# Biased scores in SBUF with one minimum per half tile, weights in three DVE passes with their low halves by the tensor engine, feed-forward six half tiles behind

## The chip, the core and the metric

The kernel runs on one core of a Trainium2 chip. A core has a tensor engine (TensorE, in the profile PE, its weight loads PEld), a vector engine (VectorE, DVE), a scalar engine (ScalarE, ACT), GpSimd (POOL) and SyncE (SP), whose queue issues all DMAs here. The metric is the device time of one execution in microseconds; each kernel is timed in several runs, and one more execution is profiled.

## What is computed

The inputs q, k and v have 8 batches, 8 heads, 576 positions and 64 values per head, in fp32. The feed-forward weights arrive as 64-bit floats.

```python
scores = scale * q @ k^T                        # scale = 1/8
scores = where(0 <= row - col < 128, scores - slope_h * |row - col|, -1e9)
attn = exp(scores - max(scores)); attn = attn / (sum(attn) + 1e-9)
x = (attn @ v), heads side by side              # 8 x 576 x 512
h = relu(x @ w_in)                              # 512 -> 1024
gate = sigmoid(3-tap convolution of h along the sequence, per channel)
out = (h * gate) @ w_out                        # 1024 -> 512
```

## The kernel before

All 8 x 576 positions lie in one row of 4608 and are cut into 36 tiles of 128. Two tiles make a chunk of 256 columns for the feed-forward, so there are 18 chunks. Heads come in two units u of four; "half tile" stands for one unit of a tile in the attention, and for one of the two slots of an iteration in the feed-forward.

Attention, per tile t and unit u. `qkT` transposes q and k on TensorE (`pt`) and copies them out (L219). `scores` multiplies them in plain fp32 into two PSUM banks `sc`, against the tile itself and the tile before. DVE folds the two together by mask copies (L246; in tiles that contain a batch boundary two more of them per bank), and then, head by head, one fused instruction (L261) scales by -1/8, adds the bias in place in PSUM and leaves the row minimum in `st`. ScalarE reads the bank, takes the exponential into `e` and leaves its sum (L271). DVE adds 1e-9, inverts (L279, L280) and scales `e` (L281). `attnT` transposes `e` on TensorE (`pa`), ScalarE copies it out (L291), GpSimd cuts it into the parts for this tile and the one before (L294, L297). `av` of tile t - 1 runs one iteration later; its result is split into a rounded high half `x[:,0]` (L323, ScalarE) and a low half `x[:,1]` (L324, DVE). `xfin` then copies one column between neighbouring chunks, since the convolution reaches one position to each side: for an even tile the first column of the new chunk into the last column of the chunk before (L338), for an odd tile the other way (L340).

Feed-forward, per chunk and pair of 128-channel blocks (four such items per chunk, 72 in all). `up` multiplies x by w_in in three products of halves into banks `p`, 24 matmuls; ScalarE and DVE make relu, convolution and gate (`hh`, `z`, L365 to L380), then `gh` (L385) and `gl` (L386, GpSimd) are the halves of the result. `down` multiplies them by w_out into `o`, 12 matmuls. The banks `sc`, `pt`, `pa`, `av`, `p` share six PSUM buffers in rotation.

Weights. Each of 16 blocks of 128 x 512 (and the small convolution block) is fetched as pairs of 32-bit words into `wst` (three buffers), turned into fp32 in `wg` by `to_f32`, and split into a rounded high half (`wi[0]`, `wo[0]`, L177) and a low half (`wi[1]`, `wo[1]`, L178).

The order. TensorE's order is the order of the code (a manual schedule). The other engines' orders are made by a scheduler from priorities, and each engine then works strictly in its order. Iteration t issues: scores of tile t, `av` of tile t - 1 with `xfin`, loads, some weight blocks by the table WEIGHTS, the up of slot 2t, a down, `qkT` of tile t + 1, `pa` of unit 0, more weight blocks, the up of slot 2t + 1, `pa` of unit 1, a down. The item of slot s is number s - LAG. With LAG = 7 the first up of a chunk falls on the second slot of an odd iteration; the last column that it reads comes from the tile whose `av` stands at the head of the same iteration.

Of the kernel before, what the change touches and what calls it, by code (L numbers as in the profile page):

```python
# [8 lines left out]
F32 = mybir.dt.float32  # L9
F32R = mybir.dt.float32r  # L10
# [3 lines left out]
AF = mybir.ActivationFunctionType  # L14
ALU = mybir.AluOpType

P = 128
# [4 lines left out]
def tile_alibi_window_attention_conv_glu(  # L22
# [10 lines left out]
    nc = tc.nc  # L33
# [4 lines left out]
    HU = 4  # L38
# [8 lines left out]
    cpool = ctx.enter_context(tc.tile_pool(name="cpool", bufs=1))  # L47
# [3 lines left out]
    pst = ctx.enter_context(tc.tile_pool(name="pst", bufs=6, space=bass.MemoryType.PSUM))  # L51
    pso = ctx.enter_context(tc.tile_pool(name="pso", bufs=2, space=bass.MemoryType.PSUM))

    def as32(ap):
        return ap.bitcast(F32)


    ident_f = apool.tile([P, P], F32, name="ident_f", tag="e", bufs=2)
    make_identity(nc, ident_f)
    ident_r = cpool.tile([P, P], F32R, name="ident_r")  # L60
    nc.vector.tensor_copy(out=ident_r, in_=ident_f)
    ident = as32(ident_r)

    ones = apool.tile([P, P], F32, name="ones", tag="e", bufs=2)
    nc.vector.memset(ones, 1.0)
# [3 lines left out]
    def mask_from(name, conds):  # L69
# [19 lines left out]
        out=mh, in_=mh, pattern=[[0, P]], compare_op=ALU.is_ge, fill=0.0, base=-(P // 2), channel_multiplier=1  # L89
# [10 lines left out]
    dist = apool.tile([P, P], F32, name="dist", tag="qk", bufs=2)  # L100
    nc.gpsimd.iota(dist, pattern=[[-1, P]], base=0, channel_multiplier=1, allow_small_or_imprecise_dtypes=True)
    nc.vector.scalar_tensor_tensor(
        out=dist, in0=m_prev_f, scalar=float(P), in1=dist, op0=ALU.mult, op1=ALU.add
    )
    bias = cpool.tile([P, H, P], F32, name="bias")
    for h in range(H):
        slope = 2.0 ** (-8.0 * (h + 1) / H)
        nc.vector.tensor_scalar(
            out=bias[:, h, :], in0=dist, scalar1=-8.0 * slope, scalar2=None, op0=ALU.mult
        )  # L110


# [7 lines left out]
    WB = 512  # L120

    def to_f32(st, g):

        lo, hi = st[..., 0], st[..., 1]
        gf = g.bitcast(F32)
        nc.scalar.activation(out=g, in_=hi.bitcast(F32), func=AF.Tanh, scale=16513.0)
        nc.vector.tensor_scalar(
            out=lo, in0=lo, scalar1=29, scalar2=0x40000000, op0=ALU.logical_shift_right, op1=ALU.bitwise_or  # L130
        )
        nc.vector.tensor_scalar(
            out=hi, in0=hi, scalar1=4, scalar2=1, op0=ALU.logical_shift_left, op1=ALU.logical_shift_right
        )
        nc.vector.tensor_tensor(out=hi, in0=hi, in1=lo, op=ALU.bitwise_xor)  # L135
        nc.vector.scalar_tensor_tensor(
            out=gf, in0=hi.bitcast(F32), scalar=3.0e38, in1=g, op0=ALU.min, op1=ALU.mult
        )
        return gf
# [25 lines left out]
    def convert_weight():  # L165
        block, st = fetched.pop(0)
        g = wpool.tile([P, WB], I32, name="wg", tag="wg")
        if block is None:
            n = 3 * NFC
            f = to_f32(st, g[:n, :P])  # L170
            ps = pst.tile([P, n], F32, name="pcw", tag="tr")
            nc.tensor.transpose(ps, f, ident[:n, :n])
            nc.vector.tensor_copy(out=cw.rearrange("p k f -> p (k f)"), in_=ps)
            return
        f = to_f32(st, g)
        hi, lo = block[1]
        nc.scalar.copy(out=hi, in_=f)  # L177
        nc.gpsimd.tensor_tensor(out=lo, in0=f, in1=as32(hi), op=ALU.subtract)  # L178

# [2 lines left out]
    NG = HU // 2  # L184
# [36 lines left out]
    def scores(t, u):  # L221
        first = (t * P) % S
        slot = t % SLOTS
        if slot:
            win, prev, cur = slice(slot - 1, slot + 1), 0, 1
        else:
            win, prev, cur = slice(0, SLOTS, SLOTS - 1), 1, 0
        e = apool.tile([P, HU, P], F32, name=f"e{t}_{u}", tag="e", bufs=2)
        st = apool.tile([P, 3, HU], F32, name=f"st{t}_{u}", tag="st", bufs=3)

        pss = [pst.tile([P, NG, 2, P], F32, name=f"sc{t}_{u}_{a}", tag="tr") for a in range(2)]
        for g in range(NG):
            for a in range(2):
                rows = slice(a * D, (a + 1) * D)
                qt = qkT_all[rows, slot, u, 0, g, :]
                if first == 0:
                    nc.tensor.matmul(pss[a][:, g, cur], qt, qkT_all[rows, slot, u, 1, g, :], start=True, stop=True)
                else:
                    nc.tensor.matmul(pss[a][:, g], qt, qkT_all[rows, win, u, 1, g, :], start=True, stop=True)  # L239
        for a in range(2):  # L240
            ps = pss[a]
            s_cur, s_prev = ps[:, :, cur, :], ps[:, :, prev, :]
            shp = [P, 2, P]

            def put(mask, data):
                nc.vector.copy_predicated(  # L246
                    out=s_cur, mask=mask.unsqueeze(1).to_broadcast(shp), data=data
                )

            negb = neg.unsqueeze(2).to_broadcast(shp)  # L250
            if first == 0:
                put(m_prev, negb)
            else:
                put(m_prev, s_prev)
                if first + P > S:
                    put(m_half, negb)
                elif first < P:
                    put(m_after, negb)
            for g in range(NG):
                j = 2 * g + a  # L260
                nc.vector.tensor_tensor_reduce(  # L261
                    out=ps[:, g, cur, :],
                    in0=ps[:, g, cur, :],
                    in1=bias[:, u * HU + j, :],
                    scale=-0.125,
                    scalar=3.0e38,
                    op0=ALU.add,
                    op1=ALU.min,
                    accum_out=st[:, 0, j : j + 1],
                )  # L270
                nc.scalar.activation(  # L271
                    out=e[:, j, :],
                    in_=ps[:, g, cur, :],
                    func=AF.Exp,
                    bias=st[:, 0, j : j + 1],
                    scale=-1.0,
                    accum_out=st[:, 1, j : j + 1],
                )
        nc.vector.tensor_scalar(out=st[:, 2, :], in0=st[:, 1, :], scalar1=1e-9, scalar2=None, op0=ALU.add)  # L279
        nc.vector.reciprocal(out=st[:, 2, :], in_=st[:, 2, :])  # L280
        nc.vector.tensor_tensor(out=e, in0=e, in1=st[:, 2, :].unsqueeze(2).to_broadcast([P, HU, P]), op=ALU.mult)  # L281
        es[t, u] = e
# [133 lines left out]


    NFP = NFC // 2
    LAG = 7
    todo = [(c, i) for c in range(NCH) for i in range(NFP)]  # L420
    fns, downs = {}, []
    pos = 0
# [1 line left out]
    wpool = ctx.enter_context(tc.tile_pool(name="wpool", bufs=3))  # L424
    blocks = list(weight_blocks())

    WEIGHTS = [(0, 2), (1, 1), (1, 1), (1, 1), (2, 2), (2, 2), (2, 0)]

    def weight(n):
        for _ in range(n):  # L430
            if fetched:
                with tc.high_priority(WPRI):
                    convert_weight()
            if blocks:
                fetch_weight(blocks.pop(0))
# [3 lines left out]
    def up(slot):  # L439
        nonlocal pos  # L440
        if pos < len(todo) and pos + LAG <= slot:
            c, i = todo[pos]
            pos += 1
            if c not in fns:
                fns[c] = ffn_items(c)
            with tc.high_priority(-15):
                fns[c][0](i)
            downs.append((c, i))

    def down(keep=2):  # L450
        if len(downs) > keep:
            c, i = downs.pop(0)
            fns[c][1](i)
# [11 lines left out]
    with tc.manual_schedule(engines={mybir.EngineType.PE}):  # L465
        loads(0)
        for _ in range(3):
            fetch_weight(blocks.pop(0))
        loads(1)
        loadvs(0)  # L470
        for u in range(2):
            qkT(0, u)
        for t in range(NT + 2):
            if t < NT:
                with tc.high_priority(60):
                    for u in range(2):
                        scores(t, u)
            if 0 < t <= NT:
                av(t - 1)
                xfin(t - 1)  # L480
            loads(t + 2)
            loadvs(t + 1)
            wa, wb = WEIGHTS[t] if t < len(WEIGHTS) else (0, 0)
            weight(wa)
            up(2 * t)
            down()
            if t + 1 < NT:
                for u in range(2):
                    qkT(t + 1, u)
            if t < NT:  # L490
                with tc.high_priority(100):
                    attnT(t, 0)
            weight(wb)
            up(2 * t + 1)
            if t < NT:
                with tc.high_priority(100):
                    attnT(t, 1)
            down()
        while pos < len(todo):
            up(len(todo) + LAG)  # L500
            down()
        while downs:
            down(0)
# [28 lines left out]
```

## Time and profile before

| | |
|---|---|
| median of 3 runs | 690.79 us (689.79 to 690.88) |
| the profiled execution | 690.37 us |
| its span, first to last instruction | 688.6 us |
| mean granted TensorE clock | 0.960 |
| busy: PE, PEld | 630.3, 549.3 us |
| busy: DVE, ACT, POOL | 504.9, 444.8, 210.2 us |

Reading help. In the page's part 2 each digit is the busy share of a fortieth of the span, in tenths. A row of windows gives, for a stretch in us from the start, its length, each engine's busy time with the number of instructions, the granted clock (PEclk), the DMA share and the rate. A row of waits names the engine, tile and line that waited, what ended the wait, the total, the number of times and the longest. A timeline row gives start, duration, engine, line, operation, tiles, shapes and, in brackets, the idle time before it. Matmul rows run into each other, so the time from one start to the next is the time that counts. A plain fp32 matmul is recorded as two instructions.

### The profile page before, as it was taken

The page shows a single profiled execution, that of the slowest core. Times are in us where ns is not written, and L with a number is a line of the kernel's source. Part 1 is how long each engine was busy: PE and PEld are TensorE (multiplying, and loading weights), DVE is VectorE, ACT ScalarE, POOL GpSimd, SP SyncE. Part 2 cuts the span into 40 slices and gives each one's busy share as a digit, 9 for nine tenths or more (in the row PEclk, how much of TensorE's full clock was granted, in tenths as well). Part 3 has the DMA queues.
Part 4 walks back from the last instruction along what each step waited for, and adds up shares of the span by engine and source line. Part 5 has one row for each costly group of instructions (what it writes and reads, how often), then busy time and mean ns, then how long its engine had stood idle before and what let it go on. Part 6 is the DMA issues. An engine that isn't in the chain of part 4 may idle for free.

```text
span 688.6 us, 13622 instructions
## 1 busy us (share of the span) xinstructions
PE 630.3 (92%) x4833; PEld 549.3 (80%) x4833; DVE 504.9 (73%) x1584; ACT 444.8 (65%) x1258; POOL 210.2 (31%) x233
## 2 busy tenths in 40 slices
PE   3544499999999999999999999999999999999997
PEld 3333388888888888888888888888888888888996
DVE  6999887777777777777777677777777777777542
ACT  5554576766676667676667666767676667675563
POOL 1355433333232232322233333333232222323221
PEclk9566599999999999999999999999999999999999
DMA  9555322223222323222313222323222322000000
GB/s 228 140 187 164 78 47 47 79 47 78 62 62 47 79 46 79 47 77 47 93 31 78 47 77 48 78 47 78 62 62 47 79 47 77 17 31 1 31 32 30
DMA packets 120103, 47.03 MB, mean 68 GB/s; under 512 B 113356, under 2 KB 113380, under 8 KB 120036
## 3 DMA queue, kind: packets, MB, share of 16 engines
q1 hardware_dynamic: 120036, 46.17, 26.5%
q8 instruction: 38, 0.62, 0.4%
q14 instruction: 29, 0.24, 0.1%
HBM read 36.72 MB, written 9.44 MB: 67 GB/s over the span
## 4 chain that ended last, share of the span: by engine, by line
DVE 45%; PE 29%; ACT 20%; issue 3%; DMA 1%; POOL 1%; ACTq 0%; SPq 0%; DVEq 0%; POOLq 0%
DVE z L373 18%; PE p L360 11%; PE o L401 11%; DVE sc L246 7%; DVE sc L261 5%; ACT e L271 4%; ACT qkT_all L219 3%; DVE e L281 3%; ACT z L379 3%; DVE z L380 2%; PE sc L239 2%; PE av L315 2%; DVE x L324 2%; DVE wst L135 2%; ACT z L366 2%
## 5 line engine op out<-in xcount | busy, mean ns | idle before, releaser
L373 DVE SCALAR_TENSOR_TENSOR z<-hh,cw,z 128x256 f32<-128x256 f32 (+7 forms) x384 | 182.7, 518 | 96.8 <-ACT z L366 93.3
L360 PE MATMUL p<-x,wi 128*128 128x258 f32 x1728 | 230.9, 289 | 9.6 <-ACT e L271 7.6
L360 PEld LDWEIGHTS p<-x,wi 128*128 128x128 f32 x1728 | 215.5, 191 | 18.3 <-ACT e L271 11.0
L386 POOL TENSOR_TENSOR gl<-z,gh 128x512 fp32r<-128x512 f32 x72 | 92.6, 1286 | 382.7 <-ACT gh L385 339.4
L401 PE MATMUL o<-wo,gh 128*128 128x512 f32 x576 | 183.5, 400 | 0.0
L271 ACT ACTIVATE e<-sc,st 128x128 f32<-128x128 f32 x288 | 104.9, 368 | 44.6 <-DVE st L261 35.7
L379 ACT ACTIVATE z<-z 128x512 f32<-128x512 f32 x72 | 45.4, 631 | 117.4 <-DVE z L373 117.2
L401 PEld LDWEIGHTS o<-wo,gh 128*128 128x128 f32 x576 | 103.2, 188 | 19.5
L401 PE MATMUL o<-wo,gl 128*128 128x512 f32 x288 | 113.8, 395 | 0.0
L261 DVE CUSTOM_DVE_ANT_0 sc<-sc,bias 128x128 f32<-128x128 f32 x288 | 80.7, 302 | 12.2 <-ACT e L271 9.3
L380 DVE SCALAR_TENSOR_TENSOR z<-z,hh 128x512 f32<-128x512 f32 x72 | 50.1, 696 | 50.3 <-ACT z L379 50.3
L366 ACT ACTIVATE z<-hh,cw 128x256 f32<-128x256 f32 x144 | 73.8, 513 | 7.7
L288 PE MATMUL pa<-ident_r,e 128*128 128x128 f32 x288 | 46.2, 286 | 32.9 <-DVE e L281 26.0
L315 PEld LDWEIGHTS av<-rl,rv 128*64 128x64 f32 x1088 | 59.3, 138 | 13.3 <-issue 10.6
L315 PE MATMUL av<-rl,rv 128*64 128x128 f32 x1088 | 68.5, 278 | 0.9 <-POOL rl L297 0.8
L239 PE MATMUL sc<-qkT_all 64*128 64x256 f32 x512 | 68.8, 411 | 0.0
L401 PEld LDWEIGHTS o<-wo,gl 128*128 128x128 f32 x288 | 54.1, 188 | 13.0
L385 ACT CAST gh<-z 128x512 fp32r<-128x512 f32 x72 | 45.1, 627 | 29.0 <-DVE z L380 29.0
L239 PEld LDWEIGHTS sc<-qkT_all 64*128 64x128 f32 x512 | 49.9, 199 | 16.9 <-issue 10.8
L288 PEld LDWEIGHTS pa<-ident_r,e 128*128 128x128 f32 x288 | 35.0, 147 | 35.4 <-issue 7.7
L297 POOL TENSOR_SCALAR_AFFINE_SELECT rl<-rl 128x512 f32<-128x512 f32 x72 | 52.1, 724 | 35.5 <-ACT rl L291 31.3
L365 ACT ACTIVATE hh<-p 128x258 f32<-128x258 f32 x144 | 55.5, 385 | 9.0 <-PE p L360 8.5
(57 smaller groups left out, 632.1 us busy)
## 6 DMA issues: line engine op xcount, KB each, us to landing
out_dram<-ob SPq DMA_DIRECT2D x36, 256.0 KB, 2.1
rqk<-in_q_dram SPq DMA_DIRECT2D x32, 256.0 KB, 3.4
rqk<-in_k_dram SPq DMA_DIRECT2D x32, 256.0 KB, 3.8
rv<-in_v_dram SPq DMA_DIRECT2D x32, 256.0 KB, 3.0
wst<-in_moe_w_in_dram SPq DMA_DIRECT2D x8, 512.0 KB, 5.3
wst<-in_moe_w_out_dram SPq DMA_DIRECT2D x8, 512.0 KB, 3.5
rqk<-in_q_dram SPq DMA_DIRECT2D x8, 128.0 KB, 2.9
rqk<-in_k_dram SPq DMA_DIRECT2D x8, 128.0 KB, 3.2
```

Of the source, the lines that this page charges most:

```text
L239: nc.tensor.matmul(pss[a][:, g], qt, qkT_all[rows, win, u, 1, g, :], start=True, stop=True)
L261: nc.vector.tensor_tensor_reduce(out=ps[:, g, cur, :], in0=ps[:, g, cur, :], in1=bias[:, u * HU + j, :], scale=-0.125, scalar=3.0e38, op0= ...
L271: nc.scalar.activation(out=e[:, j, :], in_=ps[:, g, cur, :], func=AF.Exp, bias=st[:, 0, j : j + 1], scale=-1.0, accum_out=st[:, 1, j : j + 1],
L288: nc.tensor.transpose(ps[:, j, :], e[:, j, :], ident)
L315: nc.tensor.matmul(ps[a * D : (a + 1) * D, u * NG + g], vraw[tt][:, u * HU + j], rl[:, side, j], start=n == 0, stop=n == len(sides) - 1,)
L360: nc.tensor.matmul(ps[:, :XW], a[:, cc, f * P : (f + 1) * P], x[:, cc, :], start=n == 0, stop=n == last)
L366: nc.scalar.activation(out=z[:, ff, :], in_=hh[:, ff, 1 : 1 + CW], func=AF.Copy, scale=cw[:, 1, f : f + 1])
L373: nc.vector.scalar_tensor_tensor(out=z[:, ff, a:cut], in0=hh[:, ff, a + kk : cut + kk], scalar=cw[:, kk, f : f + 1], in1=z[:, ff, a:cut], ...
L379: nc.scalar.activation(out=z, in_=z, func=AF.Tanh)
L380: nc.vector.scalar_tensor_tensor(out=z, in0=z, scalar=1.0, in1=hh[:, :, 1 : 1 + CW], op0=ALU.add, op1=ALU.mult)
L386: nc.gpsimd.tensor_tensor(out=gl, in0=z, in1=as32(gh), op=ALU.subtract)
L401: nc.tensor.matmul(oo[m], g[:, ff, ms], w[:, f, :], start=f == 0 and n == 0, stop=f == NFC - 1 and n == 2)
```

## The change

Scores. The bias table now holds slope x distance instead of -8 times it. One scalar_tensor_tensor per bank (two heads) computes -1/8 x score + bias from PSUM into `e` in SBUF; one tensor_reduce per half tile takes the four minima; the exponentials then work in place in `e`.

Weights. `to_f32` gets a scaled copy on ScalarE (L131 of the new kernel) and has three DVE passes instead of four. The low half is no longer a subtraction on GpSimd: TensorE adds f (by the identity, in fp32) and -hi (by a negative identity, in fp32r) in a bank `pw`, and ScalarE copies it out.

Order. LAG is 6, the table WEIGHTS spreads the blocks otherwise, and the first down of an iteration stands ahead of its up.

```diff
+    nident = cpool.tile([P, P], F32R, name="nident")
+    nc.vector.tensor_scalar(out=nident, in0=ident_f, scalar1=-1.0, scalar2=None, op0=ALU.mult)
...
-        nc.scalar.activation(out=g, in_=hi.bitcast(F32), func=AF.Tanh, scale=16513.0)
-        nc.vector.tensor_scalar(
-            out=lo, in0=lo, scalar1=29, scalar2=0x40000000, op0=ALU.logical_shift_right, op1=ALU.bitwise_or
+        nc.scalar.activation(out=g, in_=hi.bitcast(F32), func=AF.Tanh, scale=1.0e9)
+        nc.scalar.activation(out=hi.bitcast(F32), in_=hi.bitcast(F32), func=AF.Copy, scale=2.0**-112)
+        nc.vector.tensor_scalar(out=lo, in0=lo, scalar1=29, scalar2=None, op0=ALU.logical_shift_right)
+        nc.vector.scalar_tensor_tensor(
+            out=hi, in0=hi, scalar=3, in1=lo, op0=ALU.logical_shift_left, op1=ALU.bitwise_or
         )
-        nc.vector.tensor_scalar(
-            out=hi, in0=hi, scalar1=4, scalar2=1, op0=ALU.logical_shift_left, op1=ALU.logical_shift_right
-        )
-        nc.vector.tensor_tensor(out=hi, in0=hi, in1=lo, op=ALU.bitwise_xor)
...
         nc.scalar.copy(out=hi, in_=f)
-        nc.gpsimd.tensor_tensor(out=lo, in0=f, in1=as32(hi), op=ALU.subtract)
+        ps = pst.tile([P, WB], F32, name="pw", tag="tr")
+        nc.tensor.matmul(ps, ident, f, start=True, stop=False)
+        nc.tensor.matmul(ps, nident, hi, start=False, stop=True)
+        nc.scalar.copy(out=lo, in_=ps)
...
-            for g in range(NG):
-                j = 2 * g + a
-                nc.vector.tensor_tensor_reduce(
-                    out=ps[:, g, cur, :],
-                    in0=ps[:, g, cur, :],
-                    in1=bias[:, u * HU + j, :],
-                    scale=-0.125,
...
-                    accum_out=st[:, 0, j : j + 1],
-                )
-                nc.scalar.activation(
-                    out=e[:, j, :],
-                    in_=ps[:, g, cur, :],
...
+            heads = e.rearrange("p (g a) k -> p a g k", a=2)[:, a]
+            b = bias[:, u * HU : (u + 1) * HU].rearrange("p (g a) k -> p a g k", a=2)[:, a]
+            nc.vector.scalar_tensor_tensor(out=heads, in0=s_cur, scalar=-0.125, in1=b, op0=ALU.mult, op1=ALU.add)
+        nc.vector.tensor_reduce(out=st[:, 0, :], in_=e, axis=mybir.AxisListType.X, op=ALU.min)
+        for j in range(HU):
+            nc.scalar.activation(
+                out=e[:, j, :],
+                in_=e[:, j, :],
...
-    LAG = 7
+    LAG = 6
...
-    WEIGHTS = [(0, 2), (1, 1), (1, 1), (1, 1), (2, 2), (2, 2), (2, 0)]
+    WEIGHTS = [(0, 2), (1, 1), (1, 0), (0, 3), (3, 2), (2, 2)]
...
             weight(wa)
+            down(1)
             up(2 * t)
-            down()
```

What moves on the engines, at the places that the prediction speaks of. First TensorE in iteration 7, where chunk 2 begins (its x is `x_699` before and `x_754` after; the numbers behind the names only count allocations). Before, behind the first slot's down:

```order
L401 MATMUL o_1_1328<-wo_113,gh_1_1233 128x512
L401 MATMUL o_1_1328<-wo_114,gh_1_1233 128x512
L401 MATMUL o_1_1328<-wo_113,gl_1_1234 128x512
L218 MATMUL pt_0_1462<-ident_r,rqk_1182 128x128 x4
L218 MATMUL pt_1_1468<-ident_r,rqk_1182 128x128 x4
L288 MATMUL pa_0_1474<-ident_r,e_0_1341 128x128 x4
L360 MATMUL p_0_1485<-x_699,wi_111 128x258 x2
```

After, the last rows of `av` of tile 6 and of the down that follows it, with the engines that a row waits for:

```order
L397 MATMUL o_0_1291<-wo_115,gh_2_1343 128x512
L397 MATMUL o_0_1291<-wo_116,gh_2_1343 128x512
L397 MATMUL o_0_1291<-wo_115,gl_2_1344 128x512
L397 MATMUL o_1_1292<-wo_115,gh_2_1343 128x512
L397 MATMUL o_1_1292<-wo_116,gh_2_1343 128x512
L397 MATMUL o_1_1292<-wo_115,gl_2_1344 128x512
L356 MATMUL p_0_1510<-x_754,wi_113 128x258 [waits DVE_49,Activation_49]
```

The first up of the chunk, p_0, moved from behind the transposes and pa of its iteration to right behind the first down.

Second, DVE in the same iteration, up to the copy of the column that this up reads. Before:

```order
L261 ISA sc_1_0_1364,st_1_1363<-sc_1_0_1364,bias 128x128
L261 ISA st_1_1363 128x1
L281 TENSOR_TENSOR e_0_1341<-e_0_1341,st_0_1342 128x512
L261 ISA sc_1_1_1365,st_1_1363<-sc_1_1_1365,bias 128x128
L261 ISA st_1_1363 128x1
L324 TENSOR_TENSOR x_1180<-av_1383,x_1180 128x4x128
L279 TENSOR_SCALAR st_1_1363<-st_1_1363 128x4
L338 CAST x_699<-x_1180 128x8
```

After:

```order
L265 TENSOR_REDUCE st_0_1432<-e_0_1431 128x4
L249 COPY_PREDICATED sc_1_0_1453<-m_prev,sc_1_0_1453 128x2x128
L249 COPY_PREDICATED sc_1_1_1454<-m_prev,sc_1_1_1454 128x2x128
L264 SCALAR_TENSOR_TENSOR e_1_1451<-sc_1_0_1453,bias 128x2x128
L264 SCALAR_TENSOR_TENSOR e_1_1451<-sc_1_1_1454,bias 128x2x128
L265 TENSOR_REDUCE st_1_1452<-e_1_1451 128x4
L275 TENSOR_SCALAR st_0_1432<-st_0_1432 128x4
L276 RECIPROCAL st_0_1432<-st_0_1432 128x4
L277 TENSOR_TENSOR e_0_1431<-e_0_1431,st_0_1432 128x512
L320 TENSOR_TENSOR x_1284<-av_1471,x_1284 128x4x128
L334 CAST x_754<-x_1284 128x8
```

The copy (L338, now L334) stays behind the scores of both units and the scaling of the first.

Third, TensorE at the end of iteration 0. Before:

```order
L218 MATMUL pt1_0_195<-ident_r_78,rqk1_131 128x128 x4
L218 MATMUL pt1_1_201<-ident_r_78,rqk1_131 128x128 x4
L288 MATMUL pa0_0_207<-ident_r_78,e0_0_148 128x128 x4
L288 MATMUL pa0_1_235<-ident_r_78,e0_1_169 128x128 x4
L239 MATMUL sc1_0_0_245<-qkT_all_116 128x256
```

After:

```order
L284 MATMUL pa0_0_207<-ident_r_78,e0_0_150 128x128 x4
L179 MATMUL pw_222<-wg_215,ident_r_78 128x512
L180 MATMUL pw_222<-wi0_113,nident_80 128x512
L179 MATMUL pw_235<-wg_228,ident_r_78 128x512
L180 MATMUL pw_235<-wi0_113,nident_80 128x512
L284 MATMUL pa0_1_241<-ident_r_78,e0_1_170 128x128 x4
L242 MATMUL sc1_0_0_251<-qkT_all_118 128x256
```

The products of the first two weight blocks stand between the two units' transposes. The other fourteen stand in iterations 1 (two), 3 (three), 4 (five) and 5 (four); the first up stands in iteration 3, behind `av` of tile 2.

More of the change, by code (lines that the diff above doesn't have):

```diff
@@ L108, in tile_alibi_window_attention_conv_glu @@
         nc.vector.tensor_scalar(
-            out=bias[:, h, :], in0=dist, scalar1=-8.0 * slope, scalar2=None, op0=ALU.mult
+            out=bias[:, h, :], in0=dist, scalar1=slope, scalar2=None, op0=ALU.mult
         )
@@ L258, in scores @@
                     put(m_after, negb)
-            for g in range(NG):
-                j = 2 * g + a
-                nc.vector.tensor_tensor_reduce(
-                    out=ps[:, g, cur, :],
-                    in0=ps[:, g, cur, :],
-                    in1=bias[:, u * HU + j, :],
-                    scale=-0.125,
-                    scalar=3.0e38,
-                    op0=ALU.add,
-                    op1=ALU.min,
-                    accum_out=st[:, 0, j : j + 1],
-                )
-                nc.scalar.activation(
-                    out=e[:, j, :],
-                    in_=ps[:, g, cur, :],
[L274 to L278, printed above, removed]
+            heads = e.rearrange("p (g a) k -> p a g k", a=2)[:, a]
[6 more added lines that the diff above has]
+                in_=e[:, j, :],
+                func=AF.Exp,
+                bias=st[:, 0, j : j + 1],
+                scale=-1.0,
+                accum_out=st[:, 1, j : j + 1],
+            )
         nc.vector.tensor_scalar(out=st[:, 2, :], in0=st[:, 1, :], scalar1=1e-9, scalar2=None, op0=ALU.add)
```

## The prediction

> **What bounds the kernel now.** I read the page from the top: span, busy tenths, then the stages by windows, then who waits for whom.
>
> ```profile
> span 688.6 us, 13622 instructions
> PE   3544499999999999999999999999999999999997
> DVE  6999887777777777777777677777777777777542
> ...
> core 0: us, PE busy (x) PEld busy (x) DVE busy (x) ACT busy (x) POOL busy (x), PEclk, DMA share, GB/s
> 10.00:80.80 70.80, 28.66 (x185) 20.45 (x184) 65.89 (x171) 40.11 (x111) 31.26 (x27) 0.65 0.59 167
> 80.80:102.37 21.57, 20.39 (x153) 18.37 (x153) 16.81 (x48) 13.69 (x40) 8.35 (x10) 0.89 0.17 38
> 102.37:620.17 517.80, 511.51 (x4034) 449.62 (x4033) 383.25 (x1256) 350.90 (x1020) 152.44 (x174) 1.00 0.24 60
> ...
> PE p L360 <- ACT e L271: 7.6, 10, 1.5
> PE p L360 <- DVE st L280: 2.0, 1, 2.0
> ```
>
> There are two stages. Up to 80.8 us DVE is busy 65.89 of 70.80 us and TensorE 28.66, at a granted clock of 0.65: DVE, with the weight conversion and the first attention tiles, is the bound. From there TensorE is: 511.51 of 517.80 us in the 30 tiles between the scores of tile 5 and those of tile 35. What TensorE waits for there is almost only one thing, score banks that the exponentials still read (p from e). So the change is worth what it does to the date at which TensorE becomes full, and what it puts in front of TensorE afterwards. The second was not obvious, so I took one tile apart (tile 7: TensorE, then DVE, then ScalarE).
>
> ```profile
> 136.64 2.00 PE L239 MATMUL sc<-qkT_all 64*128 64x256 f32 x16
> 138.57 1.97 PE L315 MATMUL av<-rl,rv 128*64 128x128 f32 x32
> 140.47 3.15 PE L360 MATMUL p<-x,wi 128*128 128x258 f32 x24
> 143.45 0.62 PE L401 MATMUL o<-wo,gh 128*128 128x512 f32 x2
> ...
> 146.25 1.03 PE L218 MATMUL pt<-ident_r,rqk 128*128 128x128 f32 x8
> 147.12 0.60 PE L288 MATMUL pa<-ident_r,e 128*128 128x128 f32 x4
> 147.47 1.70 PE L360 MATMUL p<-x,wi 128*128 128x258 f32 x12
> ...
> 137.62 0.69 DVE L380 SCALAR_TENSOR_TENSOR z<-z,hh 128x512 f32<-128x512 f32 x1 [0.69 <-ACT z L379]
> 138.23 0.75 DVE L246 COPY_PREDICATED sc<-m_prev,sc 128x256 f32<-128x256 uint8 x2
> 138.89 0.29 DVE L261 CUSTOM_DVE_ANT_0 sc<-sc,bias 128x128 f32<-128x128 f32 x1
> ...
> 142.14 0.69 DVE L281 TENSOR_TENSOR e<-e,st 128x512 f32<-128x512 f32 x1
> ...
> 143.28 0.69 DVE L324 TENSOR_TENSOR x<-av,x 128x512 fp32r<-128x512 f32 x1 [0.19 <-ACT x L323]
> 144.01 0.18 DVE L338 CAST x<-x 128x8 fp32r<-128x8 f32 x1
> ...
> 139.34 0.37 ACT L271 ACTIVATE e<-sc,st 128x128 f32<-128x128 f32 x1 [0.37 <-DVE st L261]
> 142.67 0.58 ACT L323 CAST x<-av 128x512 fp32r<-128x512 f32 x1
> ```
>
> From its start S = 136.64 TensorE does scores (1.93), av (1.90), one up (2.98), one down (2.80), transposes, and at 147.47 the second up, the first of a new chunk. In an odd tile that up reads the chunk's last column, which L338 copies out of the tile that av has just made. L338 ends at 144.19, 3.3 us before it is needed: hidden, today.
>
> **The change, part by part.**
>
> *Feed-forward six half tiles behind, down ahead of up (steady stage).* The first up of a chunk moves half a tile forward: its place is now right behind scores, av and one down, S + 1.93 + 1.90 + 2.80 = S + 6.63. For tile 7 that is 143.27, and L338 ended at 144.19: TensorE would stand for 0.9 us, and everything queued behind that up (transposes, pa, the next up) with it. DVE still does the copy last, behind the whole score work of the tile. I worked the same difference out for the fifteen odd tiles 7 to 35 (for 9, 19 and 27, where scores or av are half as long, the up's place is about 0.95 earlier). These are the rows of 21, the shortest wait, of 31, the longest of the full tiles, and of 35, the last:
>
> ```profile
> 378.31 2.00 PE L239 MATMUL sc<-qkT_all 64*128 64x256 f32 x16
> 385.34 0.17 DVE L338 CAST x<-x 128x8 fp32r<-128x8 f32 x1
> ...
> 549.88 2.00 PE L239 MATMUL sc<-qkT_all 64*128 64x256 f32 x16
> 559.31 0.17 DVE L338 CAST x<-x 128x8 fp32r<-128x8 f32 x1
> ...
> 620.17 2.00 PE L239 MATMUL sc<-qkT_all 64*128 64x256 f32 x16
> 629.28 0.18 DVE L338 CAST x<-x 128x8 fp32r<-128x8 f32 x1
> ```
>
> Tile 21: 385.51 - 384.94 = 0.57. Tile 31: 559.48 - 556.51 = 2.97. Tile 35: 2.66. The fifteen add up to 28.6 us if DVE's chain is as long as it is now.
>
> *One minimum per half tile.* It decides that length. From the first mask copy to the end of L338 it is now 138.23 to 144.19, 5.96 us. New chain, by distances from start to start in tile 7: two mask copies 0.66; two biased copies of 128x256 out of PSUM, not in the trace, between L261 (128 columns, 0.21) and L324 (512 columns, 0.61 from start to start), so 0.34 each, and 0.13 because the minimum needs the second one's result; the minimum over 128x512, no row, nearest L281 (0.60). That is 2.07, twice 4.14. Then sum and reciprocal 0.47, L281 0.60, L324 0.73, L338 0.18: 6.1 us. ScalarE hides under it: the exponentials start after 2.2 instead of 1.1, four of 0.35 (taken with 0.04 more each for reading SBUF), then L323's 0.58 end at 4.4, and DVE asks for that cast at 5.2. So the copy comes 0.15 later, in the three tiles with four more masked copies some 0.8 later: +4 us together. Against that, part of today's late dates come from banks that TensorE had to wait for, and these waits go. Bounds: 8.5 us (all like tile 21) to 45 (all like 27 or 31); I take 28, the sum that the rows give.
>
> The banks: scores are read out by the biased copies, about 2 us after the scores, and the up that took the bank now comes one down (2.8) later. So p no longer waits for e. (Written that early, e needs its buffer back from pa of the tile before, which lies one down ahead of the scores: no wait.) The stage holds 6.3 us of TensorE idle time by the window, and 9 if 30 tiles of 17.13 (three of them 1.8 shorter) are set against 517.8: gain 8.
>
> *Weights (first stage).* Per block of 128x512:
>
> ```profile
> L135 DVE TENSOR_TENSOR wst<-wst 128x512 uint32<-128x512 uint32 (+1 forms) x17 | 16.1, 953 | 0.1
> L136 DVE SCALAR_TENSOR_TENSOR wg<-wst,wg 128x512 f32<-128x512 f32 (+1 forms) x17 | 13.7, 812 | 0.1
> L178 POOL TENSOR_TENSOR wi<-wg,wi 128x512 fp32r<-128x512 f32 x8 | 11.1, 1384 | 9.6 <-ACT wi L177 9.6
> ...
> 12.92 0.63 PE L288 MATMUL pa<-ident_r,e 128*128 128x128 f32 x4 [2.26 <-DVE e L281]
> 17.98 1.08 PE L288 MATMUL pa<-ident_r,e 128*128 128x128 f32 x4 [4.43 <-DVE e L281]
> 37.47 3.79 PE L239 MATMUL sc<-qkT_all 64*128 64x256 f32 x16
> 80.82 5.22 PE L360 MATMUL p<-x,wi 128*128 128x258 f32 x24 [2.04 <-DVE st L280]
> 119.51 2.00 PE L239 MATMUL sc<-qkT_all 64*128 64x256 f32 x16
> ```
>
> DVE loses one pass of four and, with POOL's subtraction (1.38 us each) gone, the stretching of the two-input passes, 0.95 and 0.81 on average against 0.69 for L281 alone: about 1.6 us per block from start to start instead of 2.7. ScalarE gains a scaled copy (17 x 0.6) and a copy out of PSUM (16 x 0.58): +20 us. TensorE gains per block an fp32 product of 512 columns and an fp32r one. The fp32 rate is that of the scores: sixteen records, four times 256 columns one behind the other, in 1.93, so 0.97 for 512; an o product takes 0.23: 1.2 us, 19 in all, twice that at half clock. All 17 blocks are converted before the first up at 80.82 now; afterwards only seven stand ahead of it in DVE's order, and 12 of 16 products behind it.
>
> By hand: block 0 and 1 now stand in TensorE's order between pa of the two halves of tile 0, so the scores of tile 1 start near 22.5 (19.0 before). A tile then costs half the cold scores 1.9, DVE 4.2, exponentials 1.5, normalising 1.0, cold pa 1.1, and waits between them, 11.3, and a block on DVE, 1.6: 13 us. Scores of tile 3 at 48.5, the first up one chain later, near 58 instead of 80.8. To the scores of tile 6 TensorE did 34.5 us of work in 38.7 before (4.2 lost, half of it the cold first up, 5.22 for 2.98). Now it is 55.6: six ups 17.5, four downs 11.2, scores and av 7.7, transposes 4.9, twelve products 14.3. With the same 4.2 lost it is there at 118, not 119.5, and one up and one down (5.7) ahead; the chunk wait in tile 5 (1.5) goes off: gain 6. Bounds: 12, with 11.3 per tile, and -2, if ScalarE, near 50 of these 60 us, holds it up. Nothing is charged for the fetches: they wait for buffers in SP's queue as before, and DMA is at 0.17 after 80.8. The tail is the same work, one item shorter.
>
> **Sum**, against the profiled execution (690.37, span 688.6; the median of the runs is 690.79): 690.4 - 8 - 6 + 28 = 704.
>
> **The rivals.**
>
> *Faster, 683.* The copy comes early in all tiles, as in 21: 15 x 0.57 = 8.5, ramp 7: 690.4 - 8 - 7 + 8.5 = 683. For it: L380 of the half tile before sets the start of the chain (in tile 7 it starts at S + 0.98, the mask copies follow it), and the end of L338 moves from tile to tile, from S + 7.20 in 21 to S + 9.60 in 31. Against it: with down moved ahead, two ups stand closer together, and their z work crowds DVE, so L380 will hardly come earlier. It decides as soon as the mean wait is under 0.93 us.
>
> *The clock goes too, 720.* TensorE's pa took 0.63 after 2.26 us of idle time and 1.08 after 4.43: between them the clock halves. A wait of 3 us lies between. An up at half clock costs 2.2 more; for seven waits over 2 us (six of the fifteen, and tile 23 with its 0.8) that is 15, hence 720. The Trainium skill (TensorE: Matmul & The Clock Gate, Part 1) has the clock halved after an idle window of about 3.4 us that runs freely. By that rule waits of up to 3 us cost no clock, and the sum stays at 704. The trace agrees with the rule where it shows anything (2.26 kept, 4.43 lost). For the chance I go by the rows: the clock has stayed at 1.00 in a stage with waits of up to 1.5 us, and only the longest new ones come near 4.43.
>
> *The ramp is a loss, 715.* ScalarE and the in-order products hold TensorE in tiles 3 to 5. For it: 20 us more of ScalarE work, most of it there. Against it: 40.11 of 70.80 busy in the first stage leaves 30. Price 10 on top.
>
> **The numbers.** 704 has 0.68 (own range 694 to 712), faster 0.20, clock 0.05, ramp 0.07. 0.2% is about what a measurement of this kernel can tell. Within 0.2% lies where the first two meet, 0.05, two from the faster case and three from the forecast: faster 0.18, same 0.05, slower 0.77. The range takes in the faster case's 683 and the ramp's 715.
>
> **What would show it.** Right: TensorE's p waits for DVE (L334 of x) in odd tiles only, 15 times, about 2 us each; odd tiles 19 us, even ones 17.1; no wait of p for e; no L178; first up near 58. Wrong: p of odd tiles without a wait, or odd and even tiles alike; the first up after 66; p at half clock in the steady stage.

## The result and the profile after

The changed kernel takes 709.73 us (median of 4 runs, 708.49 to 711.97), the kernel before 690.84 (689.79 to 691.46): a ratio of 1.0279, 95% interval 1.0249 to 1.0309. The forecast was 704, slower, with a range of 683 to 715. The profiled execution took 708.49 us. Its page first (span, then the busy tenths of the engines), then its windows: up to the first up, from there to the scores of tile 6, to the scores of tile 35, and the rest.

```profile
span 706.8 us, 13247 instructions
PE   4765898999999989999999998999999989999997
DVE  6675887677776877777767687767776877787453
```

```profile
core 0: us, PE busy (x) PEld busy (x) DVE busy (x) ACT busy (x) POOL busy (x), PEclk, DMA share, GB/s
0.00:62.44 62.44, 32.69 (x213) 22.88 (x214) 43.43 (x118) 36.98 (x109) 9.32 (x19) 0.89 0.66 160
62.44:128.30 65.86, 60.05 (x373) 46.56 (x373) 48.44 (x97) 50.20 (x121) 15.96 (x17) 0.95 0.29 81
128.30:642.97 514.67, 496.90 (x3898) 435.66 (x3897) 384.70 (x931) 344.69 (x986) 157.24 (x168) 1.00 0.23 58
642.97:706.80 63.83, 58.41 (x401) 51.26 (x400) 33.11 (x63) 32.88 (x76) 14.89 (x14) 1.00 0.07 26
```

The row of nines that TensorE had from the sixth slice on now has eights in it. The first up starts at 62.44 instead of 80.82, yet the scores of tile 6 start 8.8 us later than before (128.30 against 119.51), and the 29 tiles from there to tile 35 take 514.67 us instead of 500.66, with 17.8 us in which TensorE does nothing. Who waits for whom (engine, line, what ended the wait: total, number, longest):

```profile
PE pa L284 <- DVE e L277: 10.7, 5, 3.0
PE p L356 <- DVE x L334: 9.4, 3, 7.5
PE p L356 <- ACT e L267: 8.8, 4, 2.8
PE p L356 <- DVE st L275: 8.6, 9, 1.7
```

Three of these lines are one wait. They name three releasers, L334 three times, L275 nine times and L267 four times, but each of the sixteen is the first up of a chunk, once in every odd iteration from tile 3 on except tile 5. L275 is merely the DVE instruction that stands right behind the copy L334, and whatever the row names, all sixteen ups start 0.14 to 0.15 us after L334 of their tile has ended. Tile 7, TensorE and then DVE, from the timeline:

```profile
145.42 2.00 PE L242 MATMUL sc<-qkT_all 64*128 64x256 f32 x16
147.35 1.97 PE L311 MATMUL av<-rl,rv 128*64 128x128 f32 x32
149.25 0.73 PE L397 MATMUL o<-wo,gh 128*128 128x512 f32 x2
...
153.09 3.14 PE L356 MATMUL p<-x,wi 128*128 128x258 f32 x24 [0.78 <-DVE st L275]
...
146.94 0.75 DVE L249 COPY_PREDICATED sc<-m_prev,sc 128x256 f32<-128x256 uint8 x2
147.60 0.75 DVE L264 SCALAR_TENSOR_TENSOR e<-sc,bias 128x256 f32<-128x256 f32 x2
148.38 0.69 DVE L265 TENSOR_REDUCE st<-e 128x4 f32<-128x512 f32 x1
...
152.05 0.68 DVE L320 TENSOR_TENSOR x<-av,x 128x512 fp32r<-128x512 f32 x1
152.77 0.17 DVE L334 CAST x<-x 128x8 fp32r<-128x8 f32 x1
152.85 0.16 DVE L275 TENSOR_SCALAR st<-st 128x4 f32<-128x4 f32 x1
```

Scores, `av` and the one down end near S + 6.9 (S = 145.42, the start of the scores). The up starts at S + 7.67, 0.15 us after L334 has ended at 152.94. From the first mask copy to the end of L334 the new chain takes 6.00 us (146.94 to 152.94); the kernel before took 5.96.

### The profile page after: what moved, and what is told of

It reads as the page before. It is cut to its first block, busy times and chain, and to the rows that moved or that the text cites. A ratio compares the mean times of both kernels' runs of the same rounds, so it can differ in the third digit from the quotient of the medians.

```text
span 706.8 us, 13247 instructions
## 1 busy us (share of the span) xinstructions
PE 648.0 (92%) x4881; PEld 556.4 (79%) x4881; DVE 509.7 (72%) x1208; ACT 464.7 (66%) x1291; POOL 197.4 (28%) x217
## 4 chain that ended last, share of the span: by engine, by line
PE 62%; DVE 22%; ACT 12%; issue 1%; DMA 1%; SPq 0%; ACTq 0%; DVEq 0%
PE p L356 29%; PE o L397 16%; DVE z L369 5%; DVE sc L249 4%; PE av L311 4%; PE pt L221 4%; PE sc L242 4%; ACT e L267 3%; DVE e L264 3%; DVE st L265 3%; PE pa L284 3%; DVE z L376 2%; PE pw L179 2%; ACT z L375 1%; DVE e L277 1%
## 5 line engine op out<-in xcount | busy, mean ns | idle before, releaser
L356 PE MATMUL p<-x,wi 128*128 128x258 f32 x1728 | 226.2, 288 | 26.9 <-DVE x L334 9.4
L369 DVE SCALAR_TENSOR_TENSOR z<-hh,cw,z 128x256 f32<-128x256 f32 (+7 forms) x384 | 176.8, 493 | 101.3 <-ACT z L362 97.9
L356 PEld LDWEIGHTS p<-x,wi 128*128 128x128 f32 x1728 | 216.9, 192 | 36.1 <-issue 18.2
L397 PE MATMUL o<-wo,gh 128*128 128x512 f32 x576 | 187.5, 406 | 1.9 <-ACT wo L181 1.9
L267 ACT ACTIVATE e<-e,st 128x128 f32<-128x128 f32 x288 | 112.2, 391 | 64.9 <-DVE st L265 64.7
L382 POOL TENSOR_TENSOR gl<-z,gh 128x512 fp32r<-128x512 f32 x72 | 94.7, 1316 | 148.5 <-ACT gh L381 144.6
L290 POOL TENSOR_SCALAR_AFFINE_SELECT rl<-rl 128x512 f32<-128x512 f32 x64 | 45.7, 714 | 304.5 <-ACT rl L287 304.5
L376 DVE SCALAR_TENSOR_TENSOR z<-z,hh 128x512 f32<-128x512 f32 x72 | 50.2, 698 | 52.1 <-ACT z L375 52.0
L293 POOL TENSOR_SCALAR_AFFINE_SELECT rl<-rl 128x512 f32<-128x512 f32 x72 | 56.9, 790 | 47.8 <-ACT rl L287 43.5
L242 PE MATMUL sc<-qkT_all 64*128 64x256 f32 x512 | 65.4, 396 | 0.0
L242 PEld LDWEIGHTS sc<-qkT_all 64*128 64x128 f32 x512 | 47.8, 191 | 15.8 <-issue 10.8
L284 PE MATMUL pa<-ident_r,e 128*128 128x128 f32 x288 | 44.5, 278 | 14.6 <-DVE e L277 10.7
L264 DVE SCALAR_TENSOR_TENSOR e<-sc,bias 128x256 f32<-128x256 f32 x144 | 54.4, 415 | 0.1
```

Source lines behind the costliest of these rows:

```text
L264: nc.vector.scalar_tensor_tensor(out=heads, in0=s_cur, scalar=-0.125, in1=b, op0=ALU.mult, op1=ALU.add)
L267: nc.scalar.activation(out=e[:, j, :], in_=e[:, j, :], func=AF.Exp, bias=st[:, 0, j : j + 1], scale=-1.0, accum_out=st[:, 1, j : j + 1],)
L284: nc.tensor.transpose(ps[:, j, :], e[:, j, :], ident)
L293: nc.gpsimd.affine_select(out=r, in_=r, pattern=[[0, HU], [1, P]], compare_op=ALU.is_ge, fill=0.0, base=0, channel_multiplier=-1)
L356: nc.tensor.matmul(ps[:, :XW], a[:, cc, f * P : (f + 1) * P], x[:, cc, :], start=n == 0, stop=n == last)
L369: nc.vector.scalar_tensor_tensor(out=z[:, ff, a:cut], in0=hh[:, ff, a + kk : cut + kk], scalar=cw[:, kk, f : f + 1], in1=z[:, ff, a:cut], ...
```

## The experiments

All kernels are set against runs of the kernel before on the same chip. The table cuts each span at the scores of tile 6 and of tile 35. With LAG 6 one up and one down more (5.7 us) lie ahead of the first cut, so its date reads 5.7 too high beside a kernel with LAG 7, and the last part as much too low.

| kernel | to tile 6 | tiles 6 to 35 | rest | span | median of runs | ratio to before, 95% |
|---|---|---|---|---|---|---|
| before | 119.51 | 500.66 | 68.43 | 688.6 | 690.84 | |
| changed | 128.30 | 514.67 | 63.83 | 706.8 | 709.73 | 1.0249 to 1.0309 |
| a_lag7 | 119.16 | 492.03 | 67.51 | 678.7 | 679.20 | 0.9809 to 0.9853 |
| a_up_first | 133.32 | 576.99 | 68.49 | 778.8 | 780.17 | 1.1272 to 1.1315 |
| a_pool_low | 117.77 | 516.05 | 63.68 | 697.5 | 700.21 | 1.0112 to 1.0168 |
| a_no_column | 123.41 | 492.15 | 61.84 | 677.4 | 679.31 | 0.9830 to 0.9860 |
| b_order | 126.48 | 511.70 | 63.62 | 701.8 | 704.09 | 1.0181 to 1.0213 |
| b_down_first | 119.76 | 492.03 | 67.51 | 679.3 | 681.02 | 0.9854 to 0.9883 |
| b_scores | 117.55 | 500.22 | 69.53 | 687.3 | 689.00 | 0.9975 to 0.9994 |
| b_weights | 117.13 | 501.39 | 68.78 | 687.3 | 688.74 | 0.9962 to 0.9990 |
| a_lag7_pool | 113.47 | 492.02 | 67.51 | 673.0 | 674.77 | 0.9762 to 0.9791 |
| a_lag7_mix | 115.90 | 492.02 | 67.58 | 675.5 | 676.91 | 0.9791 to 0.9822 |
| best_old_table | 113.70 | 492.02 | 67.48 | 673.2 | 673.79 | 0.9745 to 0.9778 |
| best_old_scores | 111.97 | 492.02 | 67.51 | 671.5 | 673.81 | 0.9751 to 0.9780 |

The theory (A in the expectations) was that of the prediction: the changed order puts the first up of a chunk in front of the column copy. The rival at the start was a simple one: the span grew by 18.2 us and TensorE's busy time by 17.7 (630.3 to 648.0), so the new weight products could be the whole loss.

**a_lag7: the changed kernel, one half tile later.**

```diff
-    LAG = 6
+    LAG = 7
```

> The changed kernel with LAG 7 instead of 6; all else kept, the down ahead of the first up too. The first up of a chunk then falls on the second slot of an odd iteration, some 11 us after the start of the scores, when the column copy (end at 7.5 to 9.6) is long done. Theory A (the waits for the column in odd tiles, about 19.4 us by their rows and 22 by the periods, are what the change loses): all odd tiles fall to 17.1 to 17.2, the time falls by about 22 to 688 (684 to 692), under the kernel before. Theory B (the loss is the 18 us of weight products that TensorE does more; the waits are hidden elsewhere): 707 to 711.

Measured: 679.20 us, 30.5 less than the changed kernel and 1.7% under the kernel before. The windows and the waits of TensorE (its five largest):

```profile
0.00:119.16 119.16, 86.54 (x549) 63.37 (x549) 88.94 (x209) 82.31 (x222) 23.02 (x35) 0.89 0.51 129
119.16:611.19 492.03, 492.03 (x3898) 435.23 (x3897) 384.57 (x930) 338.96 (x987) 158.59 (x167) 1.00 0.25 61
611.19:678.70 67.51, 63.82 (x437) 56.42 (x436) 36.15 (x72) 36.07 (x82) 16.50 (x15) 1.00 0.06 24
```

```profile
PE pa L284 <- DVE e L277: 17.7, 6, 3.9
PE pt L221 <- DMA rqk<-in_q_dram: 4.2, 1, 4.2
PE pw L179 <- DVE wg L136: 3.3, 1, 3.3
PE pa L284 <- ACT qkT_all L222: 2.9, 1, 2.9
PE pw L180 <- ACT wo L177: 2.2, 2, 1.6
```

In the steady stage TensorE is busy for 492.03 of 492.03 us and no p waits at all. The products are all still there (PE 642.4 us busy), so they are not the whole loss. The gain is larger than expected because the start and the end gain too: of the 28.1 us that the span loses, 22.6 lie in tiles 6 to 35. The run without the column copy explains this.

**a_up_first: the wait made longer.** The up ahead of its down again, with LAG 6.

```diff
-            down(1)
             up(2 * t)
+            down()
```

> The changed kernel with the first up of an iteration ahead of its down again, LAG 6 kept. The first up of a chunk stands 2.8 us earlier in TensorE's order, at 3.8 us after the start of the scores, and the column is no earlier. Theory A (the wait is set by the up's place in the order against the column copy): every one of the fifteen odd waits grows by about 2.8, in sum 42: 745 to 755. Theory B (the weight products are the loss): 707 to 713.

Measured: 780.17 us, more than either theory said. The three wait lines of p:

```profile
PE p L356 <- DVE st L275: 33.4, 9, 4.1
PE p L356 <- ACT e L267: 19.7, 4, 5.4
PE p L356 <- DVE x L334: 19.0, 4, 7.5
```

Without the 7.45 of tile 3 and the 3.84 of tile 5 they hold 60.8 us in the odd tiles 7 to 35, 41.4 more than the 19.4 of the changed kernel: the 42 expected. But the steady stage is 85 us longer than a_lag7's. Nearly all the rest is clock: the ups behind these waits take 4.2 to 5.3 us instead of 3.0, and PEclk of the stage is 0.93:

```profile
0.00:133.32 133.32, 94.96 (x585) 72.26 (x586) 90.85 (x215) 87.17 (x230) 24.82 (x36) 0.87 0.45 115
133.32:710.31 576.99, 520.21 (x3897) 461.28 (x3896) 385.60 (x932) 347.86 (x986) 147.46 (x168) 0.93 0.21 52
```

**a_no_column: the thing waited for taken away.** The copy L334 is left out and the last column of each chunk is set to zero when the chunk is made.

```diff
-            if c == NCH - 1:
-                nc.vector.memset(as32(x[:, :, :, XW - 1 : XW]), 0.0)
+            nc.vector.memset(as32(x[:, :, :, XW - 1 : XW]), 0.0)
...
-        if r == 0 and c > 0:
-            nc.vector.tensor_copy(out=chunk(c - 1)[:, :, :, XW - 1 : XW], in_=as32(chunk(c)[:, :, :, 1:2]))
```

> The changed kernel, LAG 6, without the copy of the neighbour's first column into the last column of a chunk; that column is set to zero when the chunk is made (so the convolution's last tap there is left out). The up has nothing of the newest tile to wait for. Theory A (that copy is the wait): all odd tiles 17.1, 24.5 us less: 685 (680 to 688). Theory B (the up would wait for DVE or a bank at this place in any case): 700 to 710.

Measured: 679.31 us. TensorE's order is that of the changed kernel, LAG 6 included, and all the waits that were put down to L334, L275 and L267 at the first up are gone:

```profile
123.41:615.56 492.15, 492.15 (x3898) 435.36 (x3897) 382.58 (x930) 342.43 (x986) 156.77 (x168) 1.00 0.24 61
615.56:677.40 61.84, 58.18 (x401) 51.34 (x400) 32.99 (x62) 32.88 (x76) 14.86 (x14) 1.00 0.07 26
```

This gives the price of the wait by parts: 22.5 us in tiles 6 to 35, 2.0 in the rest (tile 35), and 4.9 at the start (128.30 to 123.41), where the up of tile 3 had waited 7.48. The expectation had left out the start.

**b_order: the order alone, on the old kernel.**

```diff
-    LAG = 7
+    LAG = 6
...
-    WEIGHTS = [(0, 2), (1, 1), (1, 1), (1, 1), (2, 2), (2, 2), (2, 0)]
+    WEIGHTS = [(0, 2), (1, 1), (1, 0), (0, 3), (3, 2), (2, 2)]
...
-            up(2 * t)
-            down()
+            down(1)
+            up(2 * t)
```

> The kernel before with the order part of the change alone: LAG 6, down ahead of up, the new table of weight blocks; old scores and old weights. Theory A: the old chain of scores is as long as the new one, so the first up of a chunk waits for the column in fifteen odd tiles here too, some 24 us; no waits for banks (8 less), ramp a few us shorter: 703 (696 to 712). Theory B (order costs nothing, products do): 685 to 691.

Measured: 704.09 us, theory A. The waits of p:

```profile
PE p L360 <- DVE st L280: 31.3, 15, 14.4
PE p L360 <- ACT e L271: 2.3, 2, 1.1
```

The odd waits appear with the old scores too, 0.71 to 2.31 us each in tiles 7 to 35, since the old chain is as long as the new one. So the order by itself makes the kernel slower; neither new scores nor new weights are needed for it. The longest wait, 14.37 us, is that of tile 3: tile 6 comes at 126.48, and less the 5.7 for LAG 6 that is 1.3 us later than before, where the expectation had the ramp a few us shorter.

**b_down_first: half of the order, on the old kernel.** LAG 7 and the old table stay; only the down moves.

```diff
-            up(2 * t)
-            down()
+            down(1)
+            up(2 * t)
```

> The kernel before with one edit: the first down of an iteration ahead of its up; LAG 7, old scores, old weights and table. Theory A (the waits for score banks go because the up that takes the bank comes 2.8 us later; with LAG 7 no up meets the column copy): 682 (680 to 685), steady stage 492. Theory B (early read-out by the biased copies is needed as well): some p waits for e stay, 686 to 691.

Measured: 681.02 us, as theory A said, with this steady stage:

```profile
119.76:611.79 492.03, 492.03 (x3898) 435.24 (x3897) 363.05 (x1219) 345.42 (x987) 158.56 (x168) 1.00 0.25 61
```

All of the 8.6 us that TensorE lost to score banks before come back from two lines moved. With b_order beside it, the whole loss of the order lies in the step from LAG 7 to LAG 6 (the table went with it in this comparison).

**b_scores: the scores alone.** Biased copies and one minimum per half tile, as in the change; nothing else.

> The kernel before with the scores part alone: biased copies to SBUF, one minimum per half tile; LAG 7, the up ahead of the down, the old table and the old weights. Theory A (the waits for score banks, 8.6 us in the steady stage, go because the biased copies read the banks out about two us after the scores): 682 (679 to 685), no p waiting for e. Theory B (they go only because a down stands between the scores and the up): the up still meets unread banks, 689 to 692.

Measured: 689.00 us, 0.2% under before: theory B. The banks are still met unread, largely in the same tiles (9, 13, 27 and 31 again), only by another line (L261 here is the biased copy):

```profile
PE pa L281 <- DVE e L274: 31.7, 7, 7.5
PE pa L281 <- DVE x L331: 11.3, 1, 11.3
PE p L353 <- DVE e L261: 4.6, 8, 0.9
```

**b_weights: the weights alone.** `to_f32` with three DVE passes and the products `pw`; old scores and order.

> The kernel before with the weights part alone: three DVE passes, low halves by TensorE; old scores, order and table. Theory A (products ahead of the first up fall into TensorE's idle time, and DVE, the bound of the first stage, is relieved; but several of the sixteen products of 1.1 us stand behind it): the first up some 8 to 12 us earlier, 7 or 8 products behind it, net 685 (680 to 692). Theory B (all 18 us of products are paid in full): 703 to 709.

Measured: 688.74 us, 0.2% under before, near the upper end of theory A's range. The first up starts at 62.26, 18.6 us earlier and not the 8 to 12 expected, and the scores of tile 6 only 2.4 earlier: what the conversion gained, TensorE spent on products that stand behind that up, and on waits for them (3.9 and 2.8 us).

**a_pool_low: the products taken out of the changed kernel.**

```diff
-        ps = pst.tile([P, WB], F32, name="pw", tag="tr")
-        nc.tensor.matmul(ps, ident, f, start=True, stop=False)
-        nc.tensor.matmul(ps, nident, hi, start=False, stop=True)
-        nc.scalar.copy(out=lo, in_=ps)
+        nc.gpsimd.tensor_tensor(out=lo, in0=f, in1=as32(hi), op=ALU.subtract)
```

> The changed kernel with the low halves of the weights by the subtraction on GpSimd again, as before the change; the three DVE passes, the order and the scores are kept. TensorE's busy time falls by some 18 us (32 fp32 and 16 fp32r records). Theory A: the waits in odd tiles stay (19 us); of the 18, some are given back because DVE's two-input passes run longer beside GpSimd: 700 (694 to 706). Theory B (the products are the whole loss): 690 to 693.

Measured: 700.21 us, as theory A said, though TensorE's busy time fell by 11.7 us (648.0 to 636.3) and not by some 18, so that the exact hit is partly luck. Tile 6 comes 10.5 us earlier, the steady stage keeps its waits (516.05). In this order, three DVE passes with GpSimd's subtraction beat three passes with products. The stretching by GpSimd's subtraction shows in one line only: L133 takes 0.87 us on average instead of 0.70. L136 takes 0.81 with it and without it, so the subtraction does not stretch that line, as the prediction had assumed it did.

Alone, the three parts are worth +14.3 us (b_order), -1.4 (b_scores) and -1.7 (b_weights), in sum +11; the whole change costs 18.9. Some 8 us thus belong to no part alone. The products are at least a part of that: in the changed kernel they cost 9.5 us against GpSimd's subtraction, while the weights part alone was a small gain.

**a_lag7_pool and a_lag7_mix: both repairs together, and a mixture** (the first four blocks' low halves on TensorE, the other twelve on GpSimd).

> The changed kernel with LAG 7 and with the low halves by GpSimd's subtraction. Theory A (the two gains add: LAG 7 took 30.5 us off the changed kernel, GpSimd's subtraction 9.5): 670 (666 to 675). Theory B (with LAG 7 the products fill idle time of TensorE that the waits of the first stage leave, so taking them away gains nothing): 677 to 681.

> As the run before it in this call, but the first four blocks keep their low halves on TensorE, which stands idle then; the other twelve go to GpSimd. Theory A (products ahead of the first up are free, and DVE is not stretched by GpSimd there): 668 (664 to 672), some 2 us under the version with all on GpSimd. Theory B (ScalarE's copy out of the bank and the in-order products cost as much as they save): the same as that version within 1 us, or slower.

Measured: 674.77 and 676.91 us. The gains do not add in full: GpSimd's subtraction is worth 9.5 us with LAG 6 and 4.4 with LAG 7. The mixture is 2.1 slower than all on GpSimd, which speaks for its theory B; its pa in tile 3 waits 11.8 us for DVE instead of 9.5, and why was not followed up.

**best_old_table and best_old_scores: what of the change is needed.** a_lag7_pool with the old table, and a_lag7_pool with the old scores.

> The fastest version so far (the changed kernel with LAG 7 and GpSimd's subtraction, 674.8) with the old table of weight blocks. Theory A (one block per half tile in tiles 2 and 3 instead of three at once shortens the wait of 9.5 us in tile 3): 671 (668 to 674). Theory B (DVE has the same work before the first up is fed, or more of it ahead): 675 to 680.

> The fastest version so far (674.8) with the old scores: fused minimum per head in PSUM. Theory A (the order removed the waits for banks, the scores part is worth what it was worth alone, 1.4 us): 676 (674 to 678). Theory B (the early read-out is what keeps the banks free): waits of p for e come back, 682 to 685.

Measured: 673.79 (673.06 to 675.07) and 673.81 us (673.71 to 673.95). The table does nothing here: the wait in tile 3 is 9.49 us instead of 9.53. The scores part does nothing either, once a down stands between scores and up. So the fastest kernels, 2.4% under the kernel before (ratios 0.9761 and 0.9765), rest on two of the change's parts: the down ahead of the up with LAG 7 kept (b_down_first, ratio 0.9869), and for some 7 us more the three passes of `to_f32`, with the low halves left on GpSimd. The table and the scores part were each left out by itself; no run leaves out both.

## Why the prediction was right, and where its terms were not

The sign and the mechanism of the steady stage were right; the sum came out 5 us short (704 forecast, 708.49 for the profiled execution, 709.73 the median). Spans, term by term, 18.2 us in all:

| term | predicted | measured | from |
|---|---|---|---|
| waits for banks | -8 | -8.6 | b_down_first: 500.66 to 492.03 |
| waits for the column, tiles 7 to 35 | +28 | +24.5 | changed kernel less a_no_column, 22.5 + 2.0 |
| ramp, with tiles 3 and 5 | -6 | +2.3 | the remainder |

*The banks.* The size was right. The prediction gave two reasons, the earlier read-out and the down in between. The second alone gives all of it (b_down_first), the first alone leaves the steady stage at 500.22 (b_scores).

*The column.* The place (odd tiles only), the cause and the length of the chain held: 6.00 us against 6.1 estimated. Some tiles were near as well: tile 7 waits 0.78 (0.9 forecast), tile 31 2.79 (2.97); tile 35 was not, 1.69 (2.66). The odd tiles 7 to 33 last 18.6 us on average, 17.5 to 21.7, the full even ones 17.1 to 17.2. The waits themselves add up to 19.4 us in their rows, not 28, because the chain starts earlier than it did: on average 1.65 us after the scores of its tile instead of 2.28 (tile 17: 2.31 instead of 3.32; tile 27: 0.88 instead of 2.82). The z work of the half tile before (L380, now L376) ends earlier, which the prediction, arguing against its rival "faster", had thought hardly possible. b_down_first, with LAG 7 and the old scores, has the same early starts (2.30 and 0.87), so they come with the moved down. Whether the waits for banks had made the old dates late, as the prediction thought, no run separates from this. A wait also costs a little more than its row: the full tiles with 0.76 to 0.78 last 18.13 to 18.19 instead of 17.11 to 17.19 without the column copy, so 0.2 to 0.3 more than the row says. In fifteen tiles that is some 3.6 us, an estimate; one up lost another 1.3 to the clock, as told below. The forecast had neither, so that 24.5 came so near to 28 is partly luck: there were fewer us of waiting, and each wait cost more.

*The ramp is the step that failed*, in sign and by about 8 us. Its bounds of -12 to +2 just missed it. Tile 6 was to come at 118 and came at 128.30; of these 10.3 us some 2.4 came back, since the up of tile 5 did not wait (1.5) and the part behind tile 35 is 0.9 shorter than forecast. The 10.3 have two pieces. First, the first up was to start at 58 and started at 62.44, and the chain of waits shows what was charged at nothing:

```profile
49.12 1.01 DVE wg L136
50.15 3.15 DMA wst<-in_moe_w_out_dram
53.30 0.03 issue
53.35 0.05 issue
53.39 0.43 DVE wst L132
...
62.12 0.18 DVE x L334
62.30 0.14 issue
62.44 1.63 PE p L356 x6
```

The row of L132 on DVE:

```profile
53.39 0.43 DVE L132 TENSOR_SCALAR wst<-wst 128x512 uint32<-128x512 uint32 x1 [1.22 <-DMA wst<-in_moe_w_out_dram]
```

A weight block's fetch waits for the buffer that L136 frees, and lands 3.15 us later; L132, which needs it, stands in DVE's strict order between the mask copies and the biased copies of tile 3, so the scores wait for a weight that nobody needs yet (1.22 us of idle time on DVE). The scores of tile 3 had themselves come 1.1 us late (49.64 instead of 48.5); the other 2 us of the 4.4 were not taken apart. Second, from the first up to tile 6 TensorE needed 65.9 us where 60 were forecast. The twelve products took 18.3 instead of 14.3, since two of them waited for a bank that the biased copies still read (2.83 us) and others ran at half clock, and the four downs 14.1 instead of 11.2, because one of them waited twice for a low half that ScalarE had not yet copied out (1.87).

The column wait of tile 3, 7.48 us, lies in the first piece. The forecast date of 58 held such a wait, since it was one chain later than the scores, but the prediction counted it in no term: its column term begins with tile 7. Without the column copy the first up starts at 55.00, and tile 6 comes 4.9 us earlier (a_no_column).

*The rivals.* "Faster" named its own point of decision, a mean wait of 0.93 us; the fifteen rows have a mean of 1.3 (19.4 / 15). "The ramp is a loss" was in part what happened: not 10 on top of the forecast, but 8 off the ramp's term, and partly by the reasons it gave, products and ScalarE's copies holding TensorE in tiles 3 to 5. "The clock goes too" happened once in the steady stage. These are the timeline rows of the two waits of 2.79 us, in tiles 13 and 31:

```profile
259.50 4.49 PE L356 MATMUL p<-x,wi 128*128 128x258 f32 x24 [2.79 <-ACT e L267]
...
580.00 3.14 PE L356 MATMUL p<-x,wi 128*128 128x258 f32 x24 [2.79 <-ACT e L267]
```

The first ran partly at half clock, the second did not. The prediction quoted the Trainium skill (TensorE: Matmul & The Clock Gate, Part 1), by whose window of about 3.4 us waits of up to 3 us cost no clock. Here the measurement differs, by 1.3 us in one of fifteen waits.

## What to carry to other kernels

On an engine that works strictly in order, moving a consumer forward costs its producer's lateness times the number of rounds: compare the new date in the queue with the date at which the last of its inputs ends, for every round, the first ones included. Where an order is changed in two ways at once, price them apart: here the same two-line swap gave 9 us with LAG 7, and one number beside it cost 30. Work that is handed to an idle engine is free only while that engine is idle; products that stand behind the first up were paid by the engine that had become the bound.

## What the runs showed of the hardware

The length of an idle time that costs the clock shows within narrow bounds. An up was timed from its start to the next start on TensorE, behind each of its waits in the changed kernel, a_pool_low, b_order and a_up_first. Behind 43 waits of 0.71 to 2.31 us it took 2.94 to 2.99 us each time. Behind four waits of 2.79 us it took 2.97 once, at a granted clock of 1.00, and 4.28, 4.31 and 4.46 us, at 0.65, 0.64 and 0.62. Behind 20 waits of 3.42 us or more (15 in tiles 7 to 35 of a_up_first, five in tiles 3 and 5) it took 4.23 to 5.30. In this kernel the edge thus lies between 2.3 and 3.4 us, and a wait close to it may go either way. It is also what a_up_first paid: its waits in tiles 7 to 33 hold 56.7 us, its steady stage is 85.0 longer than a_lag7's, and 27 of the 28 us between are the longer ups.
